# Operand tiles moved to other SBUF offsets, and three changes of the planner's order, in an attention, routing and MLP kernel

## Chip, cores and metric

One core of a Trainium2 chip. The metric is the device time of one execution in microseconds (us); lower is better.

## What is computed

Linear attention over 8 batches of 576 tokens with 8 heads of 64, then a routed layer of 8 experts with a capacity of 576 tokens each, then a dense MLP of width 2048. All of it is float32 at the interfaces.

```python
q_s = softmax(q, axis=-1); k_s = softmax(k, axis=2)          # 8 x 8 x 576 x 64
attn = q_s @ (k_s^T v)                                        # -> x: 4608 x 512
logits = x @ w_gate                                           # 4608 x 8
# tokens go to experts greedily by logit, 576 per expert
out[mask_e] = relu(x[mask_e] @ w1[e]) @ w2[e]                 # 512 -> 1024 -> 512
h = out @ w_in; g = h * clip(h + 3, 0, 6) / 6                 # 512 -> 2048
y = g @ w_out                                                 # 2048 -> 512
```

The two MLP weights arrive as float64 and are narrowed on the chip.

## The kernel before

Every large product is done in three passes of float32r matmuls: each operand is split into a high part and a remainder, and high x high, high x low and low x high are summed in PSUM. `split` makes the parts of an expert's weights (L949 to L956; L952 is the remainder), L1051 and L1056 those of the hidden layer, L1022 and L1027 those of the gathered tokens.

The program is a list of operations with engines, durations and dependences; a planner (`Sched.run`) places them greedily in time with the durations and latencies that the operations state, and what it gives is each engine's fixed order of instructions, and each DMA queue's. On the chip every engine runs its own order and waits where an operand is not there.

Three stages follow each other. **Attention** (`k_part` to `x_col`) ends with the rows `xd` in DRAM. **Routing and experts**: `phase(ph)` picks the tokens of one expert on VectorE with small matmuls between (L775, L783, L796, L909), `gather(ph)` fetches the 576 rows in five tiles of 128 or 64 tokens (GpSimd's indirect DMA at L998 into `xg`, four buffers), multiplies them by the row's scale (VectorE, L1004), transposes them (TensorE, L1017, into two PSUM buffers) and splits them into `xT` (one buffer), and `expert(ph)` runs w1 (L1047) and w2 (L1069) over two halves of 288 tokens: 384 matmuls of 288 columns each expert. `phase(ph + 1)` runs beside `expert(ph)`; its operations go ahead of the expert's where both are ready. `load_expert` streams an expert's 16 weight chunks through four `st` buffers on SyncE's queue (L978, L981). **MLP** (`block`): nine blocks of 512 tokens, each 16 steps of 12 first-layer matmuls (L1229: weights stationary, `yT` moving) and 12 second-layer matmuls (L1257: `G` stationary, weights moving), all 512 columns wide.

`conv` narrows the float64 weights in 64 chunks (loads into two `cs` buffers at L1091 and L1095, ScalarE L1104 and L1106, VectorE L1108 and L1111, GpSimd L1115, the split at L1126). The first 24 chunks go to DRAM and are read back later; the other 40 go straight into the tiles in which they are used, as these come free. `yload` fetches `yT`.

The tiles that the matmuls read come from pools that lay them one behind the other. `wu` and `wl` (4 each) and `wq` (16) hold 4096 bytes per partition and lie in `main`, behind the small constants `idxf`, `idx`, `spacer`, `three2` and `three`. Behind them in `main` come `ei`, `gi` and `ei2`, then `route` (the routing's constants), then `attn`, `moe` and `mlp` in turn at one place each; `pre` and `cv` lie at the upper end. In the compiled layout of this kernel `wu`, `wl` and `wq` start 32 bytes behind a multiple of 256, `yT`, `G` and `w8` (the 8 weight tiles of the last four steps, shown as `w`) 224 bytes behind one, `xT`, `st` and `h` 96 bytes behind one. Slices that a matmul takes as its stationary operand are 512 bytes apart.

In `gather` the planner is told when the rows are there: `GL = 5000` ns after the indirect DMA (3000 for the first expert). A chunk of `conv` may be loaded from the end of the seventh expert's routing on (`("done", E - 2)`).

Of the kernel before, what the change touches and what calls it, by code (L numbers as in the profile page):

```python
# [8 lines left out]
F32 = mybir.dt.float32  # L9
# [3 lines left out]
I32 = mybir.dt.int32  # L13
# [18 lines left out]
PQB = 2  # L32
G0 = 4
PKB = 1
GL = 5000
OB = 4
PX = 2
XSB = 4
# [175 lines left out]
def tile_attn_moe_mlp(ctx, tc, q, k, v, w_gate, w1, w2, w_in, w_out, out):  # L214
# [33 lines left out]
    def open_pool(name, **kw):  # L248
        PL[name] = tc.tile_pool(name=name, bufs=1, **kw)
        PL[name] = (PL[name], PL[name].__enter__())  # L250
# [17 lines left out]
    ctx.enter_context(tc.manual_schedule())  # L268

    def const(name, shape, dt=F32):  # L270
        return (main if name in ("idxf", "idx", "spacer", "three", "three2") else PL["route"][1]).tile(shape, dt, name=name)

    DX = DM + H
    xd = dram.tile([N, DX], F32, name="xd")
# [12 lines left out]

    ones8 = const("ones8", [128, 128], BF)
    V.memset(ones8, 1.0 / 8)
    jm = const("jm", [128, 128], I32)  # L290
    V.tensor_scalar(jm, jp, 15, None, op0=OP.bitwise_and)
    samen = const("samen", [128, 128], F16)
    V.tensor_scalar(samen, jm, 0.0, None, op0=OP.is_equal)
# [6 lines left out]
    imp = dict(allow_small_or_imprecise_dtypes=True)  # L300
    wfirst = const("wfirst", [128, E])
    P.iota(wfirst, pattern=[[-1, E]], base=E, channel_multiplier=0, **imp)
    iota = const("iota", [128, 640])
    P.iota(iota, pattern=[[1, 640]], base=0, channel_multiplier=0, **imp)
    slot = const("slot", [128, 5])
    P.iota(slot, pattern=[[128, 5]], base=0, channel_multiplier=1, **imp)
# [370 lines left out]
    def f(e):  # L677
        close_pool("ps0")
        close_pool("attn")
        open_pool("psM", space=PSUM, side="right")  # L680
        open_pool("moe")
        open_pool("pre", side="right")
        open_pool("cv", side="right")
    sc.barrier(f, range(n_x), [("pool", x) for x in ("psM", "moe", "pre", "cv")])
# [301 lines left out]
    def gather(ph):  # L986
        XT = ("xT", ph)
        xn = buf(XT, "moe", [128, 2, HP, 640], "xT", 1, F32R)
        for t in range(5):
            gk = ("xg", ph, t)  # L990
            gn = buf(gk, "moe", [128, DX], "xg", XG)


            c = slice(64, 128) if ph % 2 and t == 0 else slice(0, 64) if ph % 2 == 0 and t == 4 else slice(0, 128)
            o, n = 128 * t + c.start, c.stop - c.start

            def f(e, t=t, gn=gn, c=c):
                P.indirect_dma_start(out=gn()[:c.stop], out_offset=None, in_=xd,  # L998
                                     in_offset=bass.IndirectOffsetOnAxis(ap=X["gi", ph][:c.stop, t:t + 1], axis=0))
            op("pool", 1040, f, r=[("gi", ph), "xd"], w=[gk], lat=GL if ph else 3000, prio=-1)  # L1000

            def f(e, gk=gk, c=c):
                x = X[gk][c, :DM].rearrange("p (h d) -> p h d", h=H)
                EN[e].tensor_tensor(x, x, X[gk][c, DM:, None].to_broadcast([c.stop - c.start, H, D]), op=OP.mult)  # L1004
            op("dve", dve(512), f, r=[gk], w=[gk], prio=-1)
            if ph == 0 and t == 0:


                e2 = buf("ei2", "main", [128, 16], "ei2", 1, I32)
                op("dve", 64, lambda e: V.tensor_copy(e2()[:, 0:1], X["ei", 0]), r=[("ei", 0), gk], w=["ei2"], prio=-1)  # L1010
            pk = ("ptr", ph, t)
            pn = buf(pk, "psA", [128, HP, 128], "tr", 2)

            def f(e, pn=pn, gk=gk, c=c, n=n):
                p = pn()
                for j in range(HP):
                    T.transpose(p[:, j, :n], X[gk][c, 128 * j:128 * j + 128], ident[c, c])  # L1017
            op("pe", 500, f, r=[gk], w=[pk], prio=-1)

            def f(e, t=t, o=o, n=n, pk=pk):  # L1020
                x = xn() if t == 0 else X[XT]
                S.activation(x[:, 0, :, o:o + n], X[pk][:, :, :n], AF.Copy)  # L1022
            op("act", act(4 * n), f, r=[pk], w=[XT, (XT, t)], prio=-1)

            def f(e, o=o, n=n, pk=pk):
                x = X[XT]
                V.tensor_tensor(x[:, 1, :, o:o + n], X[pk][:, :, :n], x[:, 0, :, o:o + n].bitcast(F32), op=OP.subtract)  # L1027
            op("dve", dve(4 * n, ps=True), f, r=[pk, (XT, t)], w=[XT, (XT, "lo", t)], prio=-1)
# [54 lines left out]
    def conv(c, half, direct):  # L1083
        sk = ("cs", c, half)
        sn = buf(sk, "cv", [128, 256, 2], "cs", 2, I32)
        wi, wo = w_in.bitcast(I32), w_out.bitcast(I32)

        def f(e):
            t = sn()
            if c < NFM:  # L1090
                Y.dma_start(t.rearrange("p (k a) b -> p k (a b)", k=2),  # L1091
                            wi[256 * half:256 * half + 256, 256 * c:256 * c + 256].rearrange("(k p) f -> p k f", p=128))
            else:
                r0 = 128 * (c - NFM)
                Y.dma_start(t.rearrange("p a b -> p (a b)"), wo[r0:r0 + 128, 512 * half:512 * half + 512])  # L1095
        op("dma", dma(128 * 2048), f, r=[("done", E - 2)], w=[sk], prio=CVP)
        names = [(nm, c, half) for nm in ("ca", "ct", "cl")]
        news = [buf(x, "cv", [128, 256], x[0], 2, dt) for x, dt in zip(names, (F32, I32, I32))]
        A, T_, L_ = names

        def f(e):
            S.activation(news[0](), X[sk][:, :, 1].bitcast(F32), AF.Copy, scale=2.0 ** -112)  # L1104
        op("act", act(256), f, r=[sk], w=[A], prio=CVP)
        op("act", act(256), lambda e: S.activation(news[2](), X[sk][:, :, 0].bitcast(U32), AF.Copy, scale=2.0 ** -29),  # L1106
           r=[sk], w=[L_], prio=CVP)
        op("dve", dve(256, 2), lambda e: V.tensor_scalar(news[1](), X[A].bitcast(I32), 3, None,  # L1108
                                                         op0=OP.logical_shift_left), r=[A], w=[T_], prio=CVP)

        op("dve", dve(256), lambda e: V.scalar_tensor_tensor(X[T_], X[A].bitcast(I32), -0x80000000, X[T_],  # L1111
                                                             op0=OP.bitwise_and, op1=OP.bitwise_or),
           r=[A, T_], w=[T_], prio=CVP)
        pd, pen = [("pool", pool(256)), ("dve", dve(256))], dict(dve=200, act=0, pool=0)
        op("pool", pool(256), lambda e: P.tensor_tensor(X[A].bitcast(I32), X[T_], X[L_], op=OP.add), r=[T_, L_, A], w=[A],  # L1115
           prio=CVP)
        O_, o = (("W", c), 256 * half) if direct else (("co", c, half), 0)
        new = None if not direct else W[c] if half == 0 else lambda: X[O_]
        if not direct:
            new = buf(O_, "cv", [128, 2, 256], "co", 2, F32R)  # L1120
        sub = (O_, "hi", half)
        op(hi(256), 0, lambda e: copy(e, new()[:, 0, o:o + 256], X[A]), r=[A], w=[O_, sub], prio=CVP)

        def f(e):
            t = X[O_]
            EN[e].tensor_tensor(t[:, 1, o:o + 256], X[A], t[:, 0, o:o + 256].bitcast(F32), op=OP.subtract)  # L1126
        op(pd, 0, f, r=[A, sub], w=[O_], prio=CVP, pen=pen)
        if not direct:
            op("dma", dma(128 * 2048), lambda e: Y.dma_start(wh[c][:, :, 256 * half:256 * half + 256], X[O_].bitcast(F32)),
               r=[O_], w=[("wh", c)], prio=CVP)  # L1130
# [26 lines left out]
    idx = const("idx", [128, NCOL], I32)  # L1157
    op("dve", dve(NCOL), lambda e: V.tensor_scalar(idx, idxf, -1.0, None, op0=OP.add), r=["idxf"], w=["idx"])
    spacer = const("spacer", [1, 1])

    const("three2", [128, 8])
    three = const("three", [128, 1])
    V.memset(three, 3.0)

# [16 lines left out]

    def yload(b):
        YT = ("yT", b)
        yw = buf(YT, "mlp" if b % 2 else "pre", [128, 2 * HP * SB], "yT", 1, F32R)

        def yn():
            X[YT] = yw()[:, :2 * HP * SB].rearrange("p (a d s) -> p a d s", a=2, d=HP)
            return X[YT]
        for d in range(HP):
            sk = ("ys", b, d)  # L1190
            sn = buf(sk, "pre", [128, SB], "ys", 2)
            parts, s = [], SB * b
            while s < SB * b + SB:
                n = min(SB * b + SB, (s // (2 * CAP) + 1) * 2 * CAP) - s
                parts.append((s // (2 * CAP), s % (2 * CAP), s - SB * b, n))
                s += n

            def f(e, d=d, sn=sn, parts=parts):
                t = sn()
                for i, a, o, n in parts:  # L1200
                    Y.dma_start(t[:, o:o + n], yd[i][d, :, a:a + n])
            op("dma", dma(128 * 4 * SB), f, r=[("yd", p_[0]) for p_ in parts] + [("done", E - 1)], w=[sk])

            def f(e, d=d, sk=sk):
                copy(e, (yn() if d == 0 else X[YT])[:, 0, d], X[sk])
            op(hi(SB), 0, f, r=[sk], w=[YT, (YT, d)])

            def f(e, d=d, sk=sk):
                t = X[YT]
                EN[e].tensor_tensor(t[:, 1, d], X[sk], t[:, 0, d].bitcast(F32), op=OP.subtract)  # L1210
            op(lo(SB), 0, f, r=[sk, (YT, d)], w=[YT, (YT, d)])
# [123 lines left out]
```

## Time and profile before

| | |
|---|---|
| median of 3 runs | 1521.07 us (1515.7 to 1524.34) |
| profiled execution | 1521.69 us, its span 1519.7 us |
| TensorE matmul busy | 1424.0 us (94%) |
| VectorE, ScalarE, GpSimd busy | 673.5, 441.6, 594.3 us |
| granted TensorE clock, mean | 0.978 |
| attention; routing and experts; MLP | 0 to 170 us; to 704 us; to the end |

The span is that from the first to the last instruction; 2.0 us lie outside it. A matmul's busy time is modelled and overlaps its neighbours', so the rate of a stretch is read from the starts of its rows, or from a stretch's length over its count.

### The profile page before, as it was taken

To read this page: it belongs to the slowest core of one execution; us is meant where nothing else is said; L and a number is where in the kernel's file an instruction comes from. 1 tells how busy PE (TensorE), PEld (TensorE's weight loads), DVE (VectorE), ACT (ScalarE), POOL (GpSimd) and SP (SyncE) were. 2 spreads that over 40 slices of the span, in tenths; PEclk is the share of its full clock that TensorE was granted. 3 is DMA by queue.
4 is the path that set the end of the run, shared out by engine and by line. 5 is a ranking of instruction groups with operands and counts; after the bars stand their busy time and mean duration, and the time that the engine had idled before them with its cause. 6 is when DMAs were issued, how large, how long until landed. Compare 5 with 4: busy or idle time off the path is not lost.

```text
span 1519.7 us, 23045 instructions
## 1 busy us (share of the span) xinstructions
PE 1424.0 (94%) x8738; PEld 1223.7 (81%) x8738; DVE 673.5 (44%) x1656; ACT 441.6 (29%) x855; POOL 594.3 (39%) x745
## 2 busy tenths in 40 slices
PE   5889599999989897899999999999999999999997
PEld 4678588989889897898688888888888888888886
DVE  7996668677585768874841111111111111111110
ACT  3656334233242335553422121211212121121111
POOL 6874301011010116654654353533435353353433
PEclk9999799999999998999999999999999999999999
DMA  9983535235151448767311010100101010010000
GB/s 284 250 234 109 184 103 162 63 113 157 36 159 45 134 118 272 232 211 263 109 36 47 0 56 1 56 0 3 53 0 56 1 56 0 0 42 0 28 1 28
DMA packets 130558, 140.75 MB, mean 93 GB/s; under 512 B 21264, under 2 KB 104208, under 8 KB 130448
## 3 DMA queue, kind: packets, MB, share of 16 engines
q1 hardware_dynamic: 124496, 119.73, 26.4%
q0 software_dynamic: 5952, 19.56, 3.7%
q8 instruction: 68, 1.11, 0.3%
q14 instruction: 42, 0.34, 0.1%
HBM read 104.51 MB, written 34.75 MB: 92 GB/s over the span
## 4 chain that ended last, share of the span: by engine, by line
PE 67%; DVE 13%; DMA 10%; issue 3%; POOL 3%; ACT 2%; SPq 1%; POOLq 0%; ACTq 0%; DVEq 0%
PE mm L1229 24%; PE acc L1257 23%; PE mm L1047 8%; PE mm L1069 7%; DMA st<-in_moe_w_dram 6%; PE px L619 1%; DVE m L384 1%; DVE xg L1004 1%; DVE wq L952 1%; PE pkv L520 1%; DMA ys<-yd 1%; DVE h L1056 1%; DMA cs<-in_moe_w_out_dram 1%; DVE ct L1111 1%; DVE ct L1108 1%
## 5 line engine op out<-in xcount | busy, mean ns | idle before, releaser
L1235 DVE SCALAR_TENSOR_TENSOR t<-t,mm 128x512 f32<-128x512 f32 x144 | 98.8, 687 | 552.6 <-ACT t L1234 542.3
L1234 ACT ACTIVATE t<-mm,three 128x512 f32<-128x512 f32 x144 | 98.9, 688 | 567.3 <-PE mm L1229 559.0
L501 POOL TENSOR_SCALAR G<-t 128x512 fp32r<-128x512 f32 x123 | 77.2, 628 | 376.0 <-DVE t L1235 375.9
L1257 PE MATMUL acc<-wq,G 128*128 128x512 f32 x864 | 214.7, 396 | 4.3 <-POOL G L952 3.3
L1229 PE MATMUL mm<-yT,wq 128*128 128x512 f32 x864 | 213.0, 395 | 0.0
L1257 PEld LDWEIGHTS acc<-wq,G 128*128 128x128 f32 x864 | 161.2, 188 | 47.0 <-POOL G L952 8.1
L1229 PEld LDWEIGHTS mm<-yT,wq 128*128 128x128 f32 x864 | 162.1, 188 | 38.8
L998 POOL DMA_INDIRECT xg<-xd,gi x40 | 48.1, 1202 | 347.3 <-issue 328.4
L952 POOL TENSOR_TENSOR G<-t,G 128x512 fp32r<-128x512 f32 x137 | 177.0, 1292 | 11.7 <-ACT G L497 1.5
L1047 PE MATMUL mm<-xT,wq 128*128 128x288 f32 x960 | 142.7, 304 | 2.8 <-DVE xT L1027 2.6
L1069 PE MATMUL mm<-h,wq 128*128 128x288 f32 x960 | 142.2, 304 | 0.0
L1047 PEld LDWEIGHTS mm<-xT,wq 128*128 128x128 f32 x960 | 133.1, 192 | 4.7 <-DVE xT L1027 3.4
L1069 PEld LDWEIGHTS mm<-h,wq 128*128 128x128 f32 x960 | 133.3, 193 | 0.4 <-DVE h L1056 0.3
L1229 PE MATMUL mm<-yT,w 128*128 128x512 f32 x432 | 104.1, 390 | 0.0
L1229 PEld LDWEIGHTS mm<-yT,w 128*128 128x128 f32 x432 | 81.1, 188 | 17.6
L1257 PE MATMUL acc<-w,G 128*128 128x512 f32 x384 | 92.3, 389 | 0.0
L1257 PEld LDWEIGHTS acc<-w,G 128*128 128x128 f32 x384 | 72.1, 188 | 15.2
L1051 ACT ACTIVATE h<-mm 128x288 fp32r<-128x288 f32 x128 | 51.7, 406 | 97.9 <-PE mm L1047 58.2
L1115 POOL TENSOR_TENSOR ca<-ct,cl 128x256 int32<-128x256 int32 x64 | 50.4, 789 | 38.7 <-DVE ct L1111 26.3
L1056 DVE SCALAR_TENSOR_TENSOR h<-mm,h 128x288 fp32r<-128x288 f32 x128 | 57.7, 451 | 14.2 <-ACT h L1051 13.6
L497 ACT ACTIVATE wq<-st 128x512 fp32r<-128x512 f32 x78 | 49.0, 630 | 49.9 <-DMA st<-in_moe_w_dram 48.9
L952 DVE TENSOR_TENSOR wq<-st,wq 128x512 fp32r<-128x512 f32 x76 | 52.2, 688 | 11.4 <-ACT wq L497 9.5
(239 smaller groups left out, 2189.8 us busy)
## 6 DMA issues: line engine op xcount, KB each, us to landing
st<-in_moe_w_dram SPq DMA_DIRECT2D x124, 256.0 KB
yd<-yo SPq DMA_DIRECT2D x64, 144.0 KB
xd<-xs SPq DMA_DIRECT2D x32, 260.0 KB
lk<-in_k_dram SPq DMA_DIRECT2D x16, 512.0 KB
wu<-in_v_dram SPq DMA_DIRECT2D x16, 512.0 KB
wl<-in_q_dram SPq DMA_DIRECT2D x16, 512.0 KB
cs<-in_moe_w_in_dram SPq DMA_DIRECT2D x32, 256.0 KB
cs<-in_moe_w_out_dram SPq DMA_DIRECT2D x32, 256.0 KB
```

Of the source, the lines that this page charges most:

```text
L497: S.activation(o, i, AF.Copy)
L501: P.tensor_scalar(o, i, 1.0, 0.0, op0=OP.mult, op1=OP.add)
L952: EN[e].tensor_tensor(t[:, 1], view(X[src]), t[:, 0].bitcast(F32), op=OP.subtract)
L1047: T.matmul(p[:, :HC], w[:, a, k_], X[XT][:, b_, k_, o:o + HC], start=(k_ == 0 and (a, b_) == (0, 0)), stop=(k_ == 3 and (a, b_) == (1, 0)))
L1051: op("act", act(HC), lambda e, pk=pk, hn=hn: S.activation(hn()[:, 0], X[pk][:, :HC], AF.Relu), r=[pk], w=[hk, (hk, 0)])
L1056: V.scalar_tensor_tensor(t[:, 1], X[pk][:, :HC], 0.0, t[:, 0].bitcast(F32), op0=OP.max, op1=OP.subtract)
L1069: T.matmul(p[:, :HC], w[:, a, 128 * d:128 * d + 128], h[:, b_], start=(f_ == 0 and (a, b_) == (0, 0)), stop=(f_ == NFE - 1 and (a, b_) == ...
L1115: op("pool", pool(256), lambda e: P.tensor_tensor(X[A].bitcast(I32), X[T_], X[L_], op=OP.add), r=[T_, L_, A], w=[A], prio=CVP)
L1229: T.matmul(p, w[:, a, d], X[YT][:, b_, d], start=(d == 0 and (a, b_) == (0, 0)), stop=(d == 3 and (a, b_) == (1, 0)))
L1234: op("act", act(512), lambda e: S.activation(tn(), X[pk], AF.Relu, bias=three), r=[pk], w=[tk])
L1235: op("dve", dve(512, ps=True), lambda e: V.scalar_tensor_tensor(X[tk], X[tk], 6.0, X[pk], op0=OP.min, op1=OP.mult), r=[pk, tk], w=[tk])
L1257: T.matmul(p, g[:, a, 128 * t:128 * t + 128], w[:, b_], start=(f_ == 0 and (a, b_) == (0, 0)), stop=(f_ == NFM - 1 and (a, b_) == (1, 0)))
```

## The change

- `three2` (32 bytes) is gone, `ei2` grows from 64 to 128 bytes, `jm` (512 bytes) becomes a view of `iota`'s first 128 columns, so that `iota` is written after `jm` was read, and a tile of 128 bytes opens `moe`. `yT` of the pool `pre` grows by 224 bytes.
- `GL` is 8000 instead of 5000; for the last expert the planner is told 20000.
- `conv`'s loads depend on the multiply of the seventh expert's last gathered tile (`("there", E - 2, 4)`) in place of the end of its routing.

```diff
-GL = 5000
+GL = 8000
...
-        return (main if name in ("idxf", "idx", "spacer", "three", "three2") else PL["route"][1]).tile(shape, dt, name=name)
+        return (main if name in ("idxf", "idx", "spacer", "three") else PL["route"][1]).tile(shape, dt, name=name)
...
-    jm = const("jm", [128, 128], I32)
+    iota = const("iota", [128, 640])
+    jm = iota[:, :128].bitcast(I32)
...
-    iota = const("iota", [128, 640])
...
         open_pool("moe")
+
+        PL["moe"][1].tile([128, 32], F32, name="pad")
...
-            op("pool", 1040, f, r=[("gi", ph), "xd"], w=[gk], lat=GL if ph else 3000, prio=-1)
+            op("pool", 1040, f, r=[("gi", ph), "xd"], w=[gk], lat=3000 if ph == 0 else GL if ph < E - 1 else 20000, prio=-1)
...
-            op("dve", dve(512), f, r=[gk], w=[gk], prio=-1)
+            op("dve", dve(512), f, r=[gk], w=[gk, ("there", ph, t)], prio=-1)
...
-                e2 = buf("ei2", "main", [128, 16], "ei2", 1, I32)
+                e2 = buf("ei2", "main", [128, 32], "ei2", 1, I32)
...
-        op("dma", dma(128 * 2048), f, r=[("done", E - 2)], w=[sk], prio=CVP)
+        op("dma", dma(128 * 2048), f, r=[("there", E - 2, 4)], w=[sk], prio=CVP)
...
-    const("three2", [128, 8])
...
-        yw = buf(YT, "mlp" if b % 2 else "pre", [128, 2 * HP * SB], "yT", 1, F32R)
+
+        pad = 0 if b % 2 else 56
+        yw = buf(YT, "mlp" if b % 2 else "pre", [128, 2 * HP * SB + pad], "yT", 1, F32R)
```

## Rows read from the trace of the kernel before

**Rows 1.** The page: busy us of each engine (share of the span), instructions.
```profile
PE 1424.0 (94%) x8738; PEld 1223.7 (81%) x8738; DVE 673.5 (44%) x1656; ACT 441.6 (29%) x855; POOL 594.3 (39%) x745
```
**Rows 2.** Stretches: length, busy us (count) of PE, PEld, DVE, ACT, POOL, clock, DMA.
```profile
377.60:385.40 7.80, 3.77 (x26) 2.77 (x26) 7.14 (x16) 4.55 (x10) 0.95 (x1) 1.00 0.62 213
385.94:389.35 3.41, 3.41 (x19) 3.27 (x18) 2.06 (x5) 0.41 (x1) 0.00 (x0) 0.50 0.00 0
577.10:583.90 6.80, 5.77 (x23) 4.53 (x24) 6.68 (x12) 3.35 (x8) 2.48 (x3) 0.50 0.92 266
1138.25:1149.13 10.88, 10.88 (x49) 9.01 (x48) 1.38 (x2) 1.38 (x2) 3.81 (x4) 1.00 0.00 0
1166.36:1188.68 22.32, 22.32 (x98) 18.04 (x96) 2.75 (x4) 2.75 (x4) 7.65 (x8) 1.00 0.00 1
```
**Rows 3.** Timeline of PE, MLP: start us, us, engine line op out<-in, count.
```profile
1138.25 2.88 PE L1257 MATMUL acc<-w,G 128*128 128x512 f32 x12
1140.97 2.88 PE L1229 MATMUL mm<-yT,w 128*128 128x512 f32 x12
...
1166.36 2.96 PE L1257 MATMUL acc<-wq,G 128*128 128x512 f32 x12
1169.16 2.96 PE L1229 MATMUL mm<-yT,wq 128*128 128x512 f32 x12
```
**Rows 4.** Groups of PE instructions by line and operands: count, busy us, mean ns.
```profile
L1229 PE MATMUL mm<-yT,w 128*128 128x512 f32 x432 | 104.1, 390 | 0.0
...
L1229 PE MATMUL mm<-yT,wl 128*128 128x512 f32 x216 | 53.3, 395 | 0.0
```
**Rows 5.** Timeline of PE about the change from the third to the fourth expert.
```profile
366.71 9.04 PE L1069 MATMUL mm<-h,wq 128*128 128x288 f32 x66
375.59 0.32 PE L775 MATMUL rt<-oh,ge 128*128 128x64 bf16 x5
...
379.36 0.46 PE L1017 MATMUL tr<-ident,xg 64*128 64x64 f32 x4 [1.78 <-DVE xg L1004]
...
380.61 1.04 PE L1069 MATMUL mm<-h,wq 128*128 128x288 f32 x6
...
385.36 2.54 PE L1047 MATMUL mm<-xT,wu 128*128 128x288 f32 x11 [0.80 <-DVE xT L1027]
```
**Rows 6.** Timeline of DVE in that stretch.
```profile
377.90 0.69 DVE L952 TENSOR_TENSOR wq<-st,wq 128x512 fp32r<-128x512 f32 x1 [0.60 <-ACT wq L497]
378.62 1.41 DVE L1004 TENSOR_TENSOR xg<-xg 64x512 f32<-64x512 f32 x2
...
380.46 0.69 DVE L952 TENSOR_TENSOR wq<-st,wq 128x512 fp32r<-128x512 f32 x1 [0.30 <-ACT wq L497]
...
384.02 0.69 DVE L952 TENSOR_TENSOR wq<-st,wq 128x512 fp32r<-128x512 f32 x1
```
**Rows 7.** What PE waited for, in total: us, times, longest us.
```profile
PE tr L1017 <- DVE xg L1004: 16.5, 12, 3.7
```
**Rows 8.** Timeline of PE about the last expert's first transposes.
```profile
598.93 0.66 PE L1017 MATMUL tr<-ident,xg 64*128 64x64 f32 x4 [3.74 <-DVE xg L1004]
```
**Rows 9.** Timeline of SyncE's queue: the first float64 load, the forty-first, the next.
```profile
565.35 0.43 SPq L1091 DMA_DIRECT2D cs<-in_moe_w_in_dram  x1
...
689.37 0.38 SPq L1091 DMA_DIRECT2D cs<-in_moe_w_in_dram  x1
...
713.28 0.43 SPq L1091 DMA_DIRECT2D cs<-in_moe_w_in_dram  x1
```
**Rows 10.** Timeline of DVE: the seventh expert's last gathered tile.
```profile
582.53 1.78 DVE L1004 TENSOR_TENSOR xg<-xg 64x512 f32<-64x512 f32 x1
```
**Rows 11.** Timeline of the first microseconds: `iota`, the reader of `jm`, GpSimd's first wait.
```profile
1.15 0.66 POOL L304 IOTA iota<- 128x640 f32 x1
...
2.35 0.23 DVE L293 TENSOR_SCALAR samen<-jm 128x128 f16<-128x128 int32 x1
...
16.79 1.26 POOL L436 TENSOR_TENSOR s<-lk 128x512 f32<-128x512 f32 x1 [4.30 <-ACT lk L422]
```

## The prediction

> **What bounds the kernel now.** Read the busy times of the page first: TensorE's matmuls take 94% of the span, DVE, ACT and POOL less than half of it each [rows 1]. So the time is TensorE's rate and its gaps, and each is read from the stage it belongs to. In the MLP there are hardly any gaps: the stretches shown are full, at a granted clock of 1.00, with VectorE and ScalarE idle most of the time [rows 2]. There only the pitch of the matmuls counts. About a change of expert TensorE does have gaps: in the 7.80 us from 377.60 it is busy 3.77 us, and behind that comes a stretch at half clock (0.50, that is 1.2 of 2.4 GHz) in which 11 matmuls take 2.54 us, against the 1.5 us that 11 take at full clock (134.5 ns each, below) [rows 2, 5]. The attention is left as it is.
>
> The rate of the MLP depends on which tile the weights are in. Twelve matmuls with weights in `w` take 2.72 us (1140.97 less 1138.25), twelve with weights in `wq` 2.80 us (1169.16 less 1166.36) [rows 3]. Over longer stretches it is 48 in 10.88 us (226.7 ns) against 96 in 22.32 us (232.5 ns) [rows 2]. Same line, same shape, same clock; what differs is the place of the tile. `w` starts 224 bytes behind a multiple of 256, as `yT` and `G` do; `wq`, `wu` and `wl` start 32 bytes behind one. `wl` goes with `wq` (mean 395 against 390) [rows 4]. I read this as a cost that arises where the moving operand of a matmul and the stationary one that is loaded beside it stand at different offsets within 256 bytes.
>
> **The change, part by part.**
>
> *Tile places, MLP.* Adding up the tiles: without `three2`, `wu` starts at 16896 = 66 x 256; with `ei2` at 128 bytes `route` starts at 115456 = 451 x 256, so `yT`, `G` and `w8` of `mlp`, whose sizes are multiples of 256, do too; 224 bytes more bring the `yT` of `pre` there. All MLP operands then have one offset. Of 16 steps 12 hold their weights in `wq`, `wu` or `wl`: 9 x 12 x 24 = 2592 of 3456 matmuls. At 232.5 less 226.7 ns each that is 2592 x 5.8 ns = 15 us, all on the path, since TensorE has no gap there [rows 2]. Nothing in this trace has an operand at a multiple of 256, so the price there is unknown: upper bound 233.3 ns (2.80 us by 12, the new place being no better than the worst, gain 0); lower bound 213.3 ns, one column per cycle at 2.4 GHz (estimate from the granted clock), that is 3456 x 13.4 ns = 46 us more. I take 226.7, the nearest row: a common offset.
>
> The Trainium skill speaks against this part: "TensorE: Matmul & The Clock Gate", Part 2, step 1, says that TensorE reads the moving and the stationary operand through two ports of their own, so that loading the next weights takes nothing from the running matmul. By it the places would not matter and this part would be 0 instead of 15 us. The trace disagrees: 2.72 against 2.80 us.
>
> *Tile places, experts.* The 3072 matmuls of 288 columns run at 134.5 ns (66 in 8.88 us, 366.71 to 375.59, five small matmuls among them) [rows 5]. Afterwards weights start at multiples of 256, `xT` and `h` too, but the second token half of `xT` and the low part of `h` are 1152 bytes further, 128 off. Half of L1047 and two thirds of L1069 (768 + 1024 = 1792) get a common offset. No row shows a 288-column matmul with one. Bounds: 0, and 134.5 less 120 ns (288 columns at 2.4 GHz) on all, 45 us. I scale the MLP's 5.8 ns by 288/512, the nearest row: 3.3 ns x 1792 = 6 us. Of that the routing, whose small matmuls stand between in TensorE's order, may hold some back: 4 us.
>
> *`GL`.* TensorE's first transpose waits for VectorE's multiply (1.78 us at 379.36) [rows 5]; 16.5 us in all [rows 7]. But the multiply itself is not late because of rows: it starts 0.03 us behind a weight split that ended at 378.59 and had waited for ScalarE (377.90 + 0.69, then 378.62) [rows 6]. So what is late is VectorE's queue, behind weight chunks. A later planned time moves the multiply behind one more split (380.46 to 381.15 [rows 6]), 2.5 us later, and the transposes behind the last six matmuls (380.61, 1.04 us [rows 5]). What helps is that TensorE's work is moved about 3 us against the routing, once, since the planner's period is that of the routing; the wait of 1.8 us then becomes about 1.8 + 2.5 - 3 = 1.3 us. Over the six later experts that is 3 us. Bounds: all 16.5 us of waits go [rows 7] and with them six half-clock stretches (11 matmuls in 2.54 us instead of 1.48 at 134.5 ns: 1.1 us or more each), 23 us; or each change loses the 1.04 us of cover and 2.5 us of wait, 6 x 3.5 = 21 us.
>
> *The last expert at 20000.* Its transposes leave the place at which TensorE waits 3.74 us [rows 8]. What comes behind them in the old order is the seventh expert's own work, which needs nothing from them, so it moves up. I count 4 us gained. Late next: `xT` cannot be written before the seventh expert has read it, so they lose nothing. Bounds: 0 and 8 us (two half-clock stretches like that at 577.10 besides [rows 2]).
>
> *The float64 loads.* They wait for the multiply at 582.53 instead of the routing's end; the first is at 565.35 now [rows 9, 10], so they start some 18 us later. The wait stands in SyncE's queue, with the last expert's weight loads behind it. It costs little: after the forty-first chunk the next waits from 689.37 to 713.28 for free tiles [rows 9], a slack of 24 us, more than the 18 by which the first is later. In exchange the seventh expert's rows and weights have the DMA engines (0.92 busy at 577.10 [rows 2]) and VectorE to themselves. I count 4 us, bounds -10 and 10 us.
>
> *`iota`* waits for the reader of `jm` (ends 2.58, start 1.15 now): what GpSimd does behind it comes 1.5 us later, and GpSimd is idle for 4.30 us before 16.79, where it waits for ScalarE [rows 11]. Cost 0; if that cover went, 1.5 us.
>
> **Sum**, against the profiled execution: 1521.7 - 15 - 4 - 3 - 4 - 4 = 1491.7 us. That execution is 0.6 us above the median, so I say 1491.
>
> **Rivals.**
>
> *A. Multiples of 256 are better than any common offset.* The pitch of 226.7 ns is still 13.4 ns over the columns' own time, and offsets 32 and 224 both lie 32 off a multiple of 64. For: the pitch with equal offsets is very even, as a fixed cost of the place would be. Against: no row has it. Half of the 46 us would give 1491 - 23 = 1468; all of it, with half of what is open in the experts, 1491 - 46 - 15 = 1430. The same page of the Trainium skill, "Back-to-back issue gap", gives 512/2.4 + 2.5 = 215.8 ns; by it the MLP would have 38 us more, estimated 1453 us; no run here shows that pitch.
>
> *B. The places do nothing* (the offset was not what set `w` apart, or the tiles land elsewhere): the pitch stays and 1521.7 - 11 = 1511 us is left. Against it: the same line at two rates. The rule on the two ports of the Trainium skill, "TensorE: Matmul & The Clock Gate", Part 2, would lead here.
>
> *C. Slower: VectorE's queue decides the change of expert.* Its place is the multiply. If the new order puts it behind all three weight splits that are left (the last ends at 384.71 [rows 6]) and not behind one, it is 6.1 us later; TensorE has the 1.04 us of cover no more, and the half-clock stretches double: 6 x (6.1 + 1.04) + 6 x 1.1 = 50 us. With the 15 + 4 + 4 + 4 us of the other parts that is 1521.7 - 27 + 50 = 1545 us; it decides against the kernel from 27 us on, 4.5 us each change. For: all the multiplies of the first tiles start right behind a split. Against: the planner puts gathered rows ahead of splits once it takes them to be there.
>
> *D. The float64 chunks end late:* the slack of 24 us is used up and the MLP's first steps wait, say 15 us: 1506 us.
>
> **How the numbers follow.** Forecast 0.55, A 0.20, B 0.12, C 0.07, D 0.06. A run can tell 0.5% (7.6 us) from no change. Faster by more: the forecast, A, D and half of B, 0.87. Within: the other half of B, 0.06. Slower: C, 0.07. The range from 1438 to 1512 takes in the forecast with its open parts, most of A, B and D; the forecast's own range is 1470 to 1508.
>
> **What would show it.** The places: twelve matmuls with `wq` at 2.72 us in the MLP (2.80 is B, under 2.65 is A), and 66 of L1069 in about 8.7 us. `GL`: the wait of the transposes for VectorE down from 16.5 us by a few us, and how many half-clock stretches are left. The last expert: no wait of 3.74 us. The float64 loads: the first one near 585, the one that waits for free tiles still at about 713 less what the experts gained. It would be wrong above all if the pitch of the MLP lies elsewhere than 226.7 ns.

## The result, and the profile after

| | before | after |
|---|---|---|
| median | 1522.70 us | 1502.91 us (1497.89 to 1508.03, 4 runs) |
| ratio to before, as estimated from all runs | | 0.9876, 95% interval 0.9827 to 0.9925 |
| profiled execution, its span | 1521.69, 1519.7 us | 1508.03, 1505.6 us |
| routing and experts (first `mm` to last) | 511.1 us | 513.4 us |
| MLP (first matmul to last) | 806.9 us | 792.3 us |
| pitch of the 512-column matmuls, w1 and w2 side | 232.0, 230.3 ns | 226.7, 227.1 ns |
| pitch of the 288-column matmuls, w1 and w2 side | 132.5, 133.1 ns | 132.6, 133.0 ns |

The forecast of 1491 us was 12 us too low and its range of 1438 to 1512 us held the time; faster was right. The profiled execution is the slowest of the four, 5 us above their median, so the stages of it are read one by one and small sums are left to the medians. A pitch is the distance between the starts of two matmuls that follow without a gap, at the granted clock of 1.00; the table has the mean of each side, whatever tile the weights are in. Most lines of the kernel stand two further down after the change: L1017 is L1019, L952 is L954.

The MLP does what the forecast said. The stretches that answer to [rows 2, 3] (columns as there):

```profile
1133.73:1144.61 10.88, 10.88 (x50) 9.01 (x48) 2.38 (x3) 1.47 (x3) 5.38 (x6) 1.00 0.01 2
1161.69:1183.45 21.76, 21.76 (x97) 18.02 (x96) 2.75 (x4) 2.76 (x4) 7.64 (x9) 1.00 0.00 1
```

The timeline of TensorE in the same place:

```profile
1139.17 2.88 PE L1231 MATMUL mm<-yT,w 128*128 128x512 f32 x12
...
1161.69 2.88 PE L1231 MATMUL mm<-yT,wq 128*128 128x512 f32 x12
1164.41 2.88 PE L1259 MATMUL acc<-wq,G 128*128 128x512 f32 x12
```

The 96 matmuls with weights in `wq` take 21.76 us (226.7 ns each) where they took 22.32 us; twelve take 2.72 us, with `w` or with `wq`.

About a change of expert, the waits changed their place and not their sum: from 195 to 703 us TensorE waited 33.9 us before and 34.7 us after. What it waited for there, first before, then after (us in total, times, longest):

```profile
PE tr L1017 <- DVE xg L1004: 15.6, 11, 3.7
...
PE rt L783 <- DVE blk L778: 0.6, 1, 0.6
```

```profile
PE tr L1019 <- DVE xT L1029: 8.3, 5, 3.9
PE rt L785 <- DVE blk L780: 8.3, 5, 3.8
PE rt L911 <- DVE ids L903: 3.7, 3, 2.0
PE tr L1019 <- issue: 3.7, 3, 2.3
PE rt L911 <- DVE ids L904: 2.6, 5, 1.2
PE tr L1019 <- DVE xg L1006: 2.4, 5, 0.7
PE rt L798 <- DVE hit L795: 1.6, 2, 1.0
```

The transposes' wait for the multiply, 15.6 us before (16.5 us over the whole span, [rows 7]), is down to 2.4 us here and 3.2 us over the whole span. In its place the small matmuls of the routing wait (L785, L911, L798: 16.2 us, where their counterparts before waited 3.3 us). The longest of them shows why. First DVE, then TensorE, ScalarE and SyncE's queue, of after between 308 and 323 us:

```profile
312.01 0.68 DVE L954 TENSOR_TENSOR wq<-st,wq 128x512 fp32r<-128x512 f32 x1
316.30 0.69 DVE L954 TENSOR_TENSOR wq<-st,wq 128x512 fp32r<-128x512 f32 x1 [3.60 <-ACT wq L497]
316.91 0.22 DVE L780 TENSOR_TENSOR blk<-rt,colm 128x64 f16<-128x64 f32 x1
317.44 0.69 DVE L954 TENSOR_TENSOR wq<-st,wq 128x512 fp32r<-128x512 f32 x1 [0.31 <-ACT wq L497]
...
318.38 0.69 DVE L1006 TENSOR_TENSOR xg<-xg 128x512 f32<-128x512 f32 x1
```

```profile
312.15 0.32 PE L777 MATMUL rt<-oh,ge 128*128 128x64 bf16 x5 [0.61 <-DVE ge L766]
312.31 1.04 PE L1071 MATMUL mm<-h,wl 128*128 128x288 f32 x6
317.18 0.21 PE L785 MATMUL rt<-blk,samen 128*128 128x64 f16 x1 [3.83 <-DVE blk L780]
317.20 3.23 PE L1071 MATMUL mm<-h,wu 128*128 128x288 f32 x12
```

```profile
315.64 0.63 ACT L497 ACTIVATE wq<-st 128x512 fp32r<-128x512 f32 x1 [4.20 <-DMA st<-in_moe_w_dram]
316.77 0.63 ACT L497 ACTIVATE wq<-st 128x512 fp32r<-128x512 f32 x1 [0.51 <-DMA st<-in_moe_w_dram]
...
317.76 0.63 ACT L497 ACTIVATE wq<-st 128x512 fp32r<-128x512 f32 x1
```

```profile
308.94 1.45 SPq L983 DMA_DIRECT2D st<-in_moe_w_dram  x2
...
311.52 0.43 SPq L983 DMA_DIRECT2D st<-in_moe_w_dram  x1
```

Read it from the bottom up. The three chunks issued from 308.94 on are the three that ScalarE reads at 315.64, 316.77 and 317.76, in this order (each read waits for the semaphore of its own load): the first is there 6.70 us after its issue (315.64 less 308.94), the last 6.24 us (317.76 less 311.52). The plan counts 0.75 us for the transfer and 2 us until its use. So the remainder (L954) of the first of them stands at the head of VectorE's queue at 312.69 and waits 3.60 us for ScalarE's high part; `blk`, which needs the result of L777 at 312.15 and nothing later, stands behind it, and TensorE waits 3.83 us for `blk`. The half clock (0.50, 1.2 GHz) begins at 316.52, still in this wait, and lasts 6.83 us; 12 matmuls of 288 columns take 3.03 us (320.23 less 317.20) instead of 1.59:

```profile
316.52:323.35 6.83, 6.17 (x27) 6.01 (x27) 4.83 (x11) 1.91 (x4) 0.11 (x1) 0.50 0.07 25
```

The last expert and the float64 loads, of after:

```profile
611.19 0.43 PE L1019 MATMUL tr<-ident,xg 64*128 64x64 f32 x4 [2.29 <-issue]
...
612.86 0.63 PE L1019 MATMUL tr<-ident,xg 128*128 128x128 f32 x4 [1.24 <-issue]
...
638.14 1.97 PE L1019 MATMUL tr<-ident,xg 128*128 128x128 f32 x8 [3.94 <-DVE xT L1029]
```

```profile
592.16 1.10 SPq L1093 DMA_DIRECT2D cs<-in_moe_w_in_dram  x1
...
695.00 2.10 SPq L1093 DMA_DIRECT2D cs<-in_moe_w_in_dram  x2
...
715.08 0.90 SPq L1097 DMA_DIRECT2D cs<-in_moe_w_out_dram  x2
```

The wait of 3.74 us of [rows 8] is gone from its place, but it came back further on: the last expert's multiply was moved with its transposes, from 598.14 to 610.40 us, and ends at 611.09, so they wait 2.29 and 1.24 us there (the rows name no releaser; the first follows the multiply's end by 0.10 us). The first float64 load is 26.8 us later than in [rows 9], and the load that waits for free tiles is at 715.08 instead of 713.28: the slack held.

### The profile page after: what moved, and what is told of

Same layout as the page of the kernel before. It is cut to its first block, busy times and chain, and to the rows that moved or that the text cites. A ratio compares the mean times of both kernels' runs of the same rounds, so it can differ in the third digit from the quotient of the medians.

```text
span 1505.6 us, 23079 instructions
## 1 busy us (share of the span) xinstructions
PE 1412.7 (94%) x8738; PEld 1229.8 (82%) x8738; DVE 673.0 (45%) x1646; ACT 444.0 (29%) x858; POOL 600.4 (40%) x752
## 4 chain that ended last, share of the span: by engine, by line
PE 70%; DVE 12%; DMA 9%; issue 3%; POOL 3%; ACT 2%; SPq 0%; POOLq 0%; DVEq 0%; ACTq 0%
PE acc L1259 24%; PE mm L1231 23%; PE mm L1071 8%; PE mm L1049 8%; DMA st<-in_moe_w_dram 5%; PE px L619 2%; DMA wh<-co 2%; DVE m L384 1%; PE pkv L520 1%; DVE wq L954 1%; DVE xg L1006 1%; POOL out_dram L1277 1%; PE tr L1019 1%; DMA cs<-in_moe_w_in_dram 1%; DMA ys<-yd 1%
## 5 line engine op out<-in xcount | busy, mean ns | idle before, releaser
L1231 PE MATMUL mm<-yT,wq 128*128 128x512 f32 x864 | 207.2, 389 | 0.0
L954 POOL TENSOR_TENSOR G<-t,G 128x512 fp32r<-128x512 f32 x139 | 179.4, 1291 | 12.1 <-ACT G L497 1.6
L1071 PE MATMUL mm<-h,wq 128*128 128x288 f32 x960 | 143.9, 306 | 0.0
L1071 PEld LDWEIGHTS mm<-h,wq 128*128 128x128 f32 x960 | 134.7, 195 | 2.4 <-issue 2.4
L954 DVE TENSOR_TENSOR wq<-st,wq 128x512 fp32r<-128x512 f32 x76 | 51.9, 685 | 14.4 <-ACT wq L497 13.4
```

Of the source, the lines that this page charges most:

```text
L954: EN[e].tensor_tensor(t[:, 1], view(X[src]), t[:, 0].bitcast(F32), op=OP.subtract)
L1071: T.matmul(p[:, :HC], w[:, a, 128 * d:128 * d + 128], h[:, b_], start=(f_ == 0 and (a, b_) == (0, 0)), stop=(f_ == NFE - 1 and (a, b_) == ...
L1231: T.matmul(p, w[:, a, d], X[YT][:, b_, d], start=(d == 0 and (a, b_) == (0, 0)), stop=(d == 3 and (a, b_) == (1, 0)))
```

## The experiments

Each was run together with the kernel before, whose medians lie between 1522 and 1526 us, so the ratios are what is compared. Stages and waits are of one profiled execution each. The theory going in: the places give the 15 us of the MLP; the three changes of order give little, because TensorE's waits come from VectorE's queue, which stands in splits of chunks that have not landed. Rival: the order gives the rest of the gain, or the places act in another way than by a common offset.

**The places alone.** The changed kernel with `GL`, the last expert and the float64 loads as before.

```diff
-GL = 8000
+GL = 5000
-... lat=3000 if ph == 0 else GL if ph < E - 1 else 20000, prio=-1)
+... lat=GL if ph else 3000, prio=-1)
-... r=[("there", E - 2, 4)], w=[sk], prio=CVP)
+... r=[("done", E - 2)], w=[sk], prio=CVP)
```

> The places of the changed kernel with the order of the kernel before (GL 5000 for all later experts, float64 loads from the end of the seventh routing on). Theory: the places are worth 15 us, all of them in the MLP: 12 matmuls in 2.72 us whatever the weight tile, MLP 15 us shorter, the stage of the experts within 4 us of the kernel before (511 us), time 1507 us, like the changed kernel's within 5 us. Rival (the gain came from the order): the MLP is shorter but the whole is within 5 us of the kernel before.

Measured: 1509.14 us, ratio 0.9897 (0.9873 to 0.9920), 16 us less than before. MLP 794.6 us, experts 507.6 us, pitches 226.7 and 227.1 ns. The transposes' wait is still there (15.6 us before):

```profile
PE tr L1019 <- DVE xg L1006: 11.5, 10, 2.2
```

So 16 of the change's 20 us are in the places. In the profiled executions 12.3 of them are the MLP's and 3.4 the experts' stage's, whose pitch did not move; a difference of 3 us between two single executions is not more than their spread.

**The order alone.** The kernel before with the other three parts and without the places (the same three edits the other way round, and the key `("there", ph, t)` on the multiply).

> The order of the changed kernel (GL 8000, 20000 for the last expert, float64 loads behind the seventh expert's last tile) with the places of the kernel before. Theory: the order gives nothing, since the wait of the transposes for VectorE's multiply falls from 16.5 to about 3 us and the routing's small matmuls wait for VectorE some 15 us more instead: time 1521 us, within 6 us of the kernel before; the MLP keeps 2.80 us for 12 matmuls with weights in wq. Rival (the order gains 11 us as in the prediction's sum): 1511 us.

Measured: 1516.62 us, ratio 0.9946 (0.9926 to 0.9966): 8 us, between the two expectations, so neither holds. MLP 803.5 us, experts 507.2 us. The profile shows the exchange of waits again, 1.6 us for the multiply and 5.3 us for `blk`:

```profile
PE rt L783 <- DVE blk L778: 5.3, 5, 2.5
...
PE tr L1017 <- DVE xg L1004: 1.6, 4, 0.7
```

The two ratios multiplied give 0.9844, which lies in the interval of the whole change (0.9827 to 0.9925). So the order by itself is worth about 8 us, and on top of the places 3 us (0.9876 less 0.9897 of 1523), which the intervals do not tell from nothing. Where it comes from stays open: the profiled execution has 3.9 us less in the experts' stage and 3.4 us less in the MLP than that of before, and neither is accounted for here.

**`GL` alone, on the places.** The changed kernel with the last two of the three edits above, `GL` still 8000.

> The changed kernel with GL 8000 for all later experts, but the last expert at GL too and the float64 loads begun at the end of the seventh expert's routing, as in the kernel before. It stands between the version with the places alone (1509.1 us) and the changed kernel (1502.9 us). Theory: of the 6 us between these two GL gives about none, since it turned the wait of the transposes (11.5 us) into waits of the routing's small matmuls; the last expert and the float64 loads give what there is, so about 1508 us. Rival: GL gives it all, 1503 us. Of the trace: the wait of 3 to 4 us of the last expert's first transposes is there again by either, and the first float64 load starts some 25 us earlier than at 592.

Measured: 1508.49 us, ratio 0.9900 (0.9873 to 0.9928), against 0.9897 without the later `GL`: `GL` gives nothing that the intervals (4 us either way) show. What remains for the last expert and the float64 loads together is 0.9876 less 0.9900 of 1523, 4 us, and the intervals overlap. The first float64 load is at 558.04 us, 34 us earlier than in the changed kernel. The last expert's wait at its first transposes, which both expected, did not come back; the long wait for the multiply is at the seventh expert's first tile:

```profile
574.16 2.24 PE L1019 MATMUL tr<-ident,xg 128*128 128x128 f32 x8 [5.70 <-DVE xg L1006]
```

**Which offsets count.** A tile of 32 bytes in front of `mlp` and 96 bytes behind every `yT` put `G` and `w8` at 128 bytes behind a multiple of 256, `yT` at 128 (even blocks) or 32 (odd ones), with `wq`, `wu` and `wl` at 0.

```diff
+        PL["mlp"][1].tile([128, 8], F32, name="mpad")
-        pad = 0 if b % 2 else 56
+        pad = 24 if b % 2 else 24
```

> The changed kernel with the tiles of the MLP at several offsets within 256 bytes: wq, wu and wl at 0, G and w8 at 128, yT of even blocks at 128, of odd blocks at 32. Theory (what counts is whether the moving operand and the stationary one loaded beside it have the same offset): first layer, w8 with an even block 2.72 us for 12, all others (128, 32 and 96 apart) about 2.80; second layer, w8 2.72, wq 2.80. Rival (what counts is that the difference is a multiple of 64 or 128): those 128 apart take 2.72 as well, only 32 and 96 apart take 2.80.

Measured, in one run: 1519.52 us, MLP 806.5 us, as long as before the change. Two stretches (columns as in [rows 2]): weights in `w` and the other operand both at 128, then weights in `wq` at 0:

```profile
1143.96:1149.40 5.44, 5.44 (x25) 4.50 (x24) 1.69 (x2) 0.78 (x2) 3.48 (x4) 1.00 0.01 3
1166.12:1188.43 22.31, 22.31 (x98) 18.02 (x96) 2.75 (x4) 2.76 (x4) 7.68 (x9) 1.00 0.00 1
```

24 matmuls in 5.44 us are 226.7 ns, 96 in 22.31 us are 232.4 ns. Over the whole MLP, by moving operand and next stationary operand: 128 and 128 mostly 227 ns (mean 228 to 229); 32 and 0 233.0; 32 and 128 233.2; 128 and 0 232.4. So which common offset it is made no difference (0, 128 and 224 were seen), nor whether the two are 32, 64 [rows 2], 96 or 128 bytes apart: of these cases only the same offset helps, as the theory said, and the rival of multiples of 64 or 128 falls. Why the offsets matter is not shown.

**Why the 288-column matmuls gained nothing.** In the changed kernel two of the three passes are made narrower; 96 columns of their products are left out.

```diff
-        T.matmul(p[:, :HC], w[:, a, k_], X[XT][:, b_, k_, o:o + HC],
+        NW = HC if (a, b_) == (0, 0) else 192
+        T.matmul(p[:, :NW], w[:, a, k_], X[XT][:, b_, k_, o:o + NW],
```

(and the same for L1071)

> The changed kernel, with the expert matmuls of two of the three passes (low parts) 192 columns wide instead of 288; the last 96 columns of these passes are left out, so part of each product is not computed. It asks why the places did nothing to the 288-column matmuls (132.5 and 133.2 ns before, 132.6 and 133.0 ns after). Theory: the pitch there is the moving stream plus a fixed 13 ns (288/2.4 = 120 ns, measured 133), as in the MLP with equal offsets (213.3 + 13.4 = 226.7 ns), and the 6 ns of unequal offsets come only with the 512 columns. Then a 192-column matmul takes about 80 + 13 = 93 ns, and 12 in a row (4 wide, 8 narrow) 4 x 133 + 8 x 93 = 1.28 us. Rival: the pitch is set by loading the stationary operand, which is the same 128x128 in all of them. Then it stays near 133 ns, 12 take 1.59 us, and the columns, and with them a conflict with the columns' reads, cannot matter. Of the time: by the theory up to 2048 x 40 ns = 82 us less on TensorE, of which the routing beside it and the weights' transfers hold back a good part; by the rival no change.

Measured, in one run: 1482.49 us, 20 us less than the changed kernel. Twelve matmuls (4 wide, 8 narrow) take 1.42 us, where they take 1.59 at 132.5 ns each. The timeline of TensorE (the shape shown is that of the group's first):

```profile
299.74 1.57 PE L1073 MATMUL mm<-h,wu 128*128 128x288 f32 x12
301.15 1.57 PE L1073 MATMUL mm<-h,wl 128*128 128x288 f32 x12
302.57 1.57 PE L1073 MATMUL mm<-h,wu 128*128 128x288 f32 x12
```

From one narrow matmul to the next it is 88 ns, from the narrow to the wide one 112 and from the wide to the narrow one 154, on the median. So the stationary load is no floor at 133 ns, and the rival falls as it was stated. But 1.42 us is also more than the 1.28 us of the theory: with the wide ones at 132.5 a narrow one costs 111 ns, 21 ns less, where the expectation counted 40 ns for the 96 columns. Both expectations missed the size. A load that bounds the pitch somewhere below 118 ns (1.42 us by 12) is not excluded. Why the offset shows at 512 columns and not at 288 stays open.

**The weight loads planned later.** One line of `load_expert` in the changed kernel: the planner counts 4500 ns instead of 2000 from the end of a chunk's transfer to its use, for the second to the eighth expert. With the 0.75 us of the transfer that is 5.25 us. In the changed kernel 15 of the 116 chunks whose landing the trace tells took longer than this, and 109 longer than the 2.75 us planned.

```diff
-            op("dma", dma(128 * 2048), f, r=[("ev", ph)] + after, w=[sk])
+            op("dma", dma(128 * 2048), f, r=[("ev", ph)] + after, w=[sk], lat=4500 if ph else None)
```

> The changed kernel, but the planner is told that an expert's weight chunk lands 4500 ns behind its load in place of 2000 (experts 2 to 8), so the weight splits stand later in VectorE's order. Theory (VectorE's queue is held by splits whose chunk has not landed, and the routing's and the gather's steps behind them are late): the waits of TensorE for blk, hit and ids fall from 22 us to under 10, at least half of the twelve half-clock stretches about the experts go, time 10 us less than the changed kernel, 1493 us. Rival (the rows or the routing chain itself are late): waits stay, time within 5 us of the changed kernel.

Measured: **1482.23 us**, ratio 0.9720 (0.9701 to 0.9739), faster than both kernels and 11 us below the expectation. By the ratios that is 24 us less than after. The MLP is unchanged (792.6 us), the experts' stage is 485.6 us, 28 less than in the profiled execution of after, which was the slowest of its four. What DVE waited for ScalarE's part from 195 to 700 us, first after, then this kernel:

```profile
DVE wq L954 <- ACT wq L497: 13.4, 13, 3.6
...
DVE wu L954 <- ACT wu L497: 3.0, 3, 1.7
DVE wl L954 <- ACT wl L497: 2.9, 6, 1.0
```

```profile
DVE wq L954 <- ACT wq L497: 0.4, 1, 0.4
```

And TensorE in this kernel (the wait for the multiply isn't among its rows any more, that for `blk` is 0.4 us):

```profile
PE tr L1019 <- DVE xT L1029: 6.4, 4, 3.0
PE mm L1071 <- DVE h L1058: 5.1, 5, 1.6
PE mm L1049 <- DVE xT L1029: 2.8, 5, 0.7
...
PE rt L785 <- DVE blk L780: 0.4, 1, 0.4
```

The stretch from 195 to 676 us, first after, then this kernel (columns as in [rows 2]):

```profile
195.00:676.00 481.00, 445.81 (x3401) 425.94 (x3400) 344.03 (x1034) 179.19 (x397) 100.79 (x110) 0.96 0.44 136
```

```profile
195.00:676.00 481.00, 463.76 (x3605) 444.99 (x3604) 359.44 (x1079) 186.93 (x430) 117.97 (x136) 0.98 0.47 144
```

TensorE is busy 18.0 us more of the 481, and the clock is 0.98 instead of 0.96. The half-clock stretches that begin between 195 and 676 us sum to 40.9 us in after and 20.5 us here; if half of that time is lost (12 matmuls took 3.03 us instead of 1.59), it is 10 us. 18 and 10 are the 28 us of the stage.

**The same on the kernel before.** Only this line, with the old places and order.

> The kernel before, with the one thing altered that the changed kernel leaves alone: the weight loads of the second to eighth expert planned at 4500 ns. No places, GL 5000, the old start of the float64 loads. If the cause of the waits about a change of expert is VectorE's queue behind splits whose chunks have not landed, it doesn't need the places or the order: the experts' stage falls from 511 us by 22 to 30 us as it did on the changed kernel (513.4 to 485.6), the MLP stays at 807 us, and the time is 1523 - 26 = about 1497 us (1492 to 1502). Rival: the late splits only pay together with GL 8000 or the later float64 loads (their chunks take VectorE and the DMA engines in the seventh expert); then less than half of it, 1510 us or more.

Measured: 1495.72 us, ratio 0.9811 (0.9779 to 0.9843), 28 us less. Experts 485.0 us, MLP 804.8 us. The one line that the change leaves alone is worth more than the whole change, and needs neither the places nor the order: the rival falls. The sum of above comes out less exactly here: TensorE is busy 11.0 us more from 195 to 676 us (458.40 against 447.35), and the half-clock stretches fall from 34.1 to 13.7 us, 10 us by half, together 21 of the stage's 26 us. In this kernel's page the chunks' time from issue to landing can be read (KB, median us):

```profile
st<-in_moe_w_dram SPq DMA_DIRECT2D x124, 256.0 KB, 3.5
```

**What the order is worth once the queue is free.** With the late loads: `GL` back at 5000, and then also the last expert and the float64 loads as before (so the places alone and the late loads).

> The changed kernel with the weight loads of the second to eighth expert planned at 4500 ns as in the version with 1482.2 us, but GL at 5000 as in the kernel before (the last expert's 20000 and the float64 loads as in the changed kernel). Theory: what made the transposes and the routing wait was VectorE standing in a weight split whose chunk had not landed; GL moved the transposes in TensorE's order and only shifted these waits. With the splits planned late the multiply of the gathered rows is in time at GL 5000 as well: within 5 us of 1482, and the transposes' wait for the multiply under 4 us in all. Rival: the rows themselves need the 8000 (the gather takes longer than 5 us from issue to landing); then the 11.5 us of the transposes' waits of the version with GL 5000 come back, with their half-clock stretches, and the time is about 1482 + 12 to 1482 + 18 = 1494 to 1500 us.

> The version with the places alone, with the weight loads planned at 4500 ns: against the version with the late GL, the last expert's 20000 and the float64 loads' later start (1482.2 us) and the one with GL 5000 and these two (1483.0 us) it lacks all three parts of the change of order. Theory: they were aimed at waits that the weight splits made; with these gone they are worth under 3 us, so 1480 to 1486 us. Rival: the last expert and the float64 loads hold 4 to 8 us of their own (the seventh expert's rows and weights share the DMA engines with the chunks at 0.92 of their time), so 1487 to 1491 us.

Measured: 1483.01 us (ratio 0.9731, 0.9703 to 0.9759) and 1483.94 us (0.9744, 0.9720 to 0.9768), against 0.9720 with all parts. `GL` isn't needed: the transposes' wait for the multiply is 0.5 us at 5000. All three parts of the order together are worth 2 to 4 us there, which these runs do not tell from nothing; both theories hold.

**Later still.** 6500 ns instead of 4500.

> The changed kernel with the weight loads of the second to eighth expert planned at 6500 ns instead of 4500. If chunks take at most about 5.5 us from issue to landing, 4500 already takes VectorE's waits for ScalarE's high part away (0.4 us left of 19 us), and 6500 gives the same within 4 us: 1478 to 1486 us. Rival: the last misses go too and a further 5 to 10 us with the half-clock stretches that are left (20.5 us of them): 1472 to 1477 us. Other rival: four st buffers no longer cover 6500 ns, weights come too late for TensorE in the plan itself, and it is slower than 1487 us.

Measured: 1479.50 us, ratio 0.9705 (0.9674 to 0.9737): the same as at 4500 within the intervals, as the first expectation had it. The half-clock stretches between 195 and 676 us fall to 17.1 us, and 3.1 us of the transposes' waits for `xT` are left (6.4 us at 4500).

## Why the prediction was right, point by point

- **Places, MLP: 15 us forecast, 14.6 measured in the profiled run** (12.3 with the places alone). The step from [rows 2, 3] to "the moving and the stationary operand at different offsets cost 6 ns" was right, and so was the choice of 226.7 ns: a common offset of 0 (after), of 128 (the offsets' experiment) and of 224 ([rows 2]) all have it. From the pitches: 1728 times (232.0 less 226.7) and (230.3 less 227.1) ns are 14.7 us.
- **Rival A** (multiples of 256 better than any common offset) fell with that. No stretch here came under 226.7 ns. By the formula that the Trainium skill, "TensorE: Matmul & The Clock Gate", "Back-to-back issue gap", gives for an isolated matmul at full clock, 512/2.4 + 2.5, it would be an estimated 215.8 ns.
- **Rival B** (the places do nothing) fell in the MLP: the place of the next weights against that of the moving operand changes the pitch from 227 to 233 ns. The Trainium skill, "TensorE: Matmul & The Clock Gate", Part 2, step 1, says that loading the next weights takes no read bandwidth from the running matmul. The trace disagrees with what the prediction drew from this, that the places would not matter; whether it is read bandwidth that is lost is not shown.
- **Places, experts: 4 us forecast, 0 measured.** The step that failed is the scaling of the MLP's 5.8 ns by 288/512. The pitch did not move (132.5 and 133.1 to 132.6 and 133.0 ns). The lower bound given, 0, was the value. The 134.5 ns that the bounds start from hold five small matmuls of the routing, so the upper bound of 45 us was too wide as well; and half of what rival A leaves open in the experts is 20 us by these bounds, not the 15 of its sum.
- **`GL`: 3 us forecast, 0 measured, give or take 4.** The mechanism was half right. VectorE's queue was named as what is late [rows 6], and the wait on the multiply did go. But the sum counted only the multiply behind the splits. The routing's `blk` and `ids` stand in the same queue, and TensorE's small matmuls stand in TensorE's order, so moving the transposes handed the wait to them.
- **The last expert and the float64 loads: 8 us forecast, about 4 measured,** not told apart from each other, nor surely from 0. The slack of 24 us held, so rival D fell. The step that failed for the last expert is "they lose nothing": the multiply moved with the transposes, and they wait for it 12 us later.
- **Rival C** (slower through VectorE's queue) did not come as a loss. Its mechanism, VectorE's queue behind a split, was there: in the kernel before on the multiply, after the change on `blk`.
- **The sum.** 1491 was 12 us below the median after. Of these, 4 are the experts' places, 3 `GL`, about 4 the last two parts, and 1 is the median of before, which is 1522.70 with the runs since. So the MLP's term, half of the 30 us counted, carries the forecast; of the other 15 us about 4 came, and that the range held in spite of them is owed to its width. The forecast put `GL`'s place in doubt with bounds of 23 us gained and 21 lost.

What the prediction didn't ask is why the splits were waiting at all. [rows 6] show two remainders that wait for ScalarE (0.60 and 0.30 us), and behind them stands a plan that counts 2.75 us from issue to use of a chunk that takes 3.4 us in the median (before) and up to 6.70 us in the stretch above. Planning for 5.25 us was worth 28 us on the kernel before and 24 us on the changed one.

## What to carry to other kernels

Where TensorE waits for an operation that itself has waited for nothing, look one place ahead of it in its engine's queue: the operation that stands there is the one to look at, and moving the waiting one handed the wait, here, to its neighbour. Where an order is planned with latencies, compare each latency with the trace before anything is reordered; a transfer planned too short stalled, here, whatever was queued behind its readers. Where long runs of float32r matmuls alternate between two pitches, compare the offsets of the two operands within 256 bytes.

## What the runs showed of the hardware

- Matmuls of 512 columns in float32r, with a new 128x128 stationary operand each, follow each other mostly at 227 ns (226.7 ns over whole stretches) when the moving operand and the next stationary one start at the same offset within 256 bytes (0, 128 and 224 were seen), and at 232 to 233 ns on the mean when the offsets are 32, 64, 96 or 128 bytes apart. Why is not shown.
- At 288 columns the pitch is 132 to 134 ns with offsets that are equal, 64 or 128 bytes apart.
- TensorE's stalls cost more than their own length here: with the 18 us of waits that the late loads removed went 20 us at half clock (1.2 GHz), some 10 us of time.
- A weight chunk of 256 KB took 3.3 to 3.4 us in the median from its issue to its landing, and up to 6.7 us, in the two kernels.
